# A two-layer linear-attention and gated-ReLU kernel on one core: the order of its instructions as a table

## The chip, the core and the metric

The kernel runs on one core of a Trainium2 chip. The metric is the device time of one execution in microseconds (us). Five engines work side by side, each through its own queue in the order in which the program lists its instructions: TensorE (PE: matmuls and transposes; PEld is its weight load), VectorE (DVE), ScalarE (ACT), GpSimd (POOL) and SyncE (SP, which issues DMAs). Semaphores make an instruction wait for what it reads from another engine. TensorE writes to PSUM, the other operands lie in SBUF.

## The reference, cut to what matters

`x` is 2048 rows of 512 in bfloat16. Two equal layers follow one another, each an attention (A) and a gated unit (B):

```python
pq = einsum("bhsd,hdf->bhsf", q, w_phi)          # 32 heads of 16; the same for k
phi_q = concatenate([softmax(pq), softmax(-pq)]) # over the 16 features
kv  = einsum("bhsf,bhsd->bhfd", phi_k, v)
z   = einsum("bhsf->bhf", phi_k)
o   = (phi_q . kv) / ((phi_q . z) + 1e-6)
A   = o @ wo
gate = x @ W_gate; up = x @ W_up                 # 512 x 1376 each
B   = (where(gate > 0, gate, 0) * up) @ W_down
x = x + A(layernorm(x)); x = x + B(layernorm(x)) # twice, with the same weights
```

`kv` and `z` are sums over all 2048 rows, so no row's output of an attention can be formed before every row's keys are.

## The kernel before, in words

**Tiles.** The rows are 16 tiles of 128, in 4 chunks of 4 tiles. `X` stays in SBUF as [128, 16, 512]. The feature map is folded into the projection: 4 folds each give `Wk2 = wk.Wblk` and `Wq2 = wq.Wblk` (L348; their inputs are turned by TensorE for keys and by DMA, L334, for queries; L304 and L306 take the results from PSUM on ScalarE or VectorE, by letters of a table).

**A layer.** `Norm` (L367 on) normalises a chunk in groups of tiles: statistics on VectorE (L385, L387), a few small steps on GpSimd that end in a power of -0.5 (L393, L395, L442, L444), the normalisation on ScalarE (L456) or on VectorE or GpSimd (L468), and the turn of the rows, by TensorE (L477), by DMA for two tiles at once (L482) or for one (L486). In a chunk whose sums come free with the addition to `X` (L494), ScalarE squares instead (L408). `keys_values` then does per tile the keys (L637), exponentials of p and -p (L642), the values (L590), the sums over 16 features (`feature_sums`: one reduction of the whole tile L609, two of half a tile L619, or an addition on GpSimd L606 and a reduction of the half L615), a reciprocal (L651), the product with it (L657, cut between GpSimd and VectorE), and the matmuls into `kv` (L679). `build_R` (L701) spreads `kv` into a block matrix. `queries` does the same for q: L721, L725, the feature sums, a reciprocal of the second sums (L730), the product `rq` of the two sums (L732), the rescale of half the tile with it (L739, GpSimd or VectorE), and a DMA transpose on SP (L741). `attention` does per tile the matmuls called er (L758, into the kind of buffer `q`), a reciprocal (L776) and the division (L778) on VectorE, which free `q`, the turn of the quotient (L785 and L791 by DMA, L798 by TensorE), the projection with `wo` (L809) and the addition to `X`. `glu` does the remainder of 96 features (L520, L525, L527, L530), 10 slices of gate and up (L540), their evacuations and products (L546, L550, L553, L557), and the down-projection (L572) with the addition and, in layer 1, the output (L577).

**What sets the order.** Nothing is issued while the code above runs. `Plan.op` records each operation (1888 in all) with its engine, a cost, what it reads and writes, a latency `lat` and an earliest time `at`. `order` then simulates the engines: at every moment each free engine takes, of its ready operations, the one with the highest sum of rank (the longest way to the end) and bias; the bias comes from the table `RANK`, a base and a slope per kind of operation and engine. An operation flagged `long` (GpSimd's larger ones) keeps those flagged `port` (VectorE's L468, L557, L657, L739) from being placed while it runs. Buffers come from kinds with a fixed count (`ps` 6 and `q` 1 in PSUM; `b2` 32, `b4` 6, `b1` 26 and smaller ones in SBUF); an operation that needs a buffer waits in the plan until one is free. `emit` (L176 on) issues the operations in that order under a manual schedule, so that each engine's queue is fixed by it, and the semaphores follow from the data.

**Tables.** `STEP` (L817) chooses per tile or chunk by letters: which engine evacuates, which form of sums is used, how many of the 8 groups of L657 GpSimd takes, whether a turn is done by TensorE or DMA.

**Loads.** `setup` issues the first two tiles of `X` on SP and the rest of `X`, `wkv`, `wq` and `w_phi` on ACT's queue (L224 to L239). `load_weights` (L297) plans 28 pieces of `wo`, `wr`, `wg`, `wu` and `wd` on SP, none before the plan's time 13.0. `wake` (L315) puts 17 matmuls of zeros at TensorE's start. L265 builds a small 0/1 matrix by a reduction of the identity on VectorE.

Of the kernel before, what the change touches and what calls it, by code (L numbers as in the profile page):

```python
# [60 lines left out]
class Plan:  # L61
# [10 lines left out]
    def op(self, eng, occ, fn, reads=(), writes=(), holds=(), lat=0.0, at=0.0, group=None, port=False, long=False):  # L72
# [4 lines left out]
        base, slope = RANK.get(f"{o.group}.{eng}") or RANK[o.group]  # L77
        o.bias = base - slope * o.i_in
# [19 lines left out]
    def order(self):  # L98
        for o in self.ops:
            for p in o.preds:  # L100
                p.succs.append(o)
        for o in reversed(self.ops):
            o.rank = o.cost + o.lat + max([s.rank + hop(o.eng, s.eng) for s in o.succs], default=0.0)
        free = {k: [0.0] * n for k, (pool, n) in self.kinds.items()}
        engines = sorted({o.eng for o in self.ops})
        busy = {e: 0.0 for e in engines}
        ready = {e: [] for e in engines}
        for o in self.ops:
            o.wait, o.t0 = len(o.preds), o.at
            if not o.wait:  # L110
                ready[o.eng].append(o)
        seq, left, now, shut = [], len(self.ops), 0.0, 0.0
        while left:
            moved, later = False, []
            for e in engines:
                if busy[e] > now + 1e-9:
                    later.append(busy[e])
                    continue
                best = None
                for o in ready[e]:  # L120
                    if o.t0 > now + 1e-9:
                        later.append(o.t0)
                        continue
                    if o.port and shut > now + 1e-9:
                        later.append(shut)
                        continue
                    ok = True
                    need = {}
                    for b in o.bufs:
                        if b.slot is None:  # L130
                            need[b.kind] = need.get(b.kind, 0) + 1
                    for k, n in need.items():
                        got = [t for t in free[k] if t is not None]
                        if len(got) < n:
                            ok = False
                        else:
                            t = sorted(got)[n - 1]
                            if t > now + 1e-9:
                                later.append(t)
                                ok = False  # L140
                    if ok and (best is None or (o.rank + o.bias, -o.i) > (best.rank + best.bias, -best.i)):
                        best = o
                if best is None:
                    continue
                o = best
                ready[e].remove(o)
                moved, left = True, left - 1
                o.start, end = now, now + o.cost
                busy[e] = now + o.occ
                if o.long:  # L150
                    shut = end
                later.append(busy[e])
                for b in o.bufs:
                    if b.slot is None:
                        b.slot = min((i for i, t in enumerate(free[b.kind]) if t is not None),
                                     key=lambda i: free[b.kind][i])
                        free[b.kind][b.slot] = None
                        b.end = 0.0
                    b.left -= 1
                    b.end = max(b.end, end + o.lat + FREE)  # L160
                    if not b.left:
                        free[b.kind][b.slot] = b.end
                for s in o.succs:
                    s.wait -= 1
                    s.t0 = max(s.t0, end + o.lat + hop(e, s.eng))
                    if not s.wait:
                        ready[s.eng].append(s)
                seq.append(o)
            if not moved:
                later = [t for t in later if t > now + 1e-9]  # L170
                assert later, "the plan is stuck"
                now = min(later)
        self.seq = seq
        return seq
# [15 lines left out]
WF_IN, WK_IN, WV_IN, WQ_IN, LOADED = 3.5, 5.9, 8.6, 13.1, 13.0  # L190
X_IN = [3.25, 3.8] + [7.0] * 2 + [10.1] * 4 + [11.6] * 4 + [14.5] * 4
# [8 lines left out]
def setup(ctx, tc, A_x, A_wqkv, A_w_phi, A_wo, B_W_gate, B_W_up, B_W_down, out):  # L200
# [64 lines left out]
    nc.vector.tensor_reduce(out=st.M4[:], in_=ident[:].rearrange("p (k h) -> p h k", h=4), axis=AX.X, op=Alu.max)  # L265
    st.Wblk = const.tile([P, NDB, P], BF16, name="Wblk")
# [24 lines left out]
def load_weights(st):  # L291

    nc, seen = st.nc, {}
    for n, (name, dst, src, kb) in enumerate(st.loads):
        i = seen[name] = seen.get(name, -1) + 1
        st.pl.rank("ld" if name == "wd" else "l", n)
        st.pl.op("SP", max(0.45, kb / 245.0), lambda dst=dst, src=src: nc.sync.dma_start(out=dst, in_=src), writes=[(name, i)], at=LOADED, lat=2.0)  # L297
# [635 lines left out]
```

## Time and profile before

| | us |
|---|---|
| median of 3 runs (lowest to highest) | 382.19 (382.05 to 382.74) |
| the profiled execution's own time | 380.87 |
| its span | 379.1 |
| TensorE busy | 368.0 |
| VectorE busy | 272.1 |
| ScalarE busy | 211.0 |
| GpSimd busy | 139.5 |

The span runs from the first to the last instruction of the program in the trace; the execution's own time has 1.77 us more around it. The profiled execution is one run, and it lies below the three timed ones. "L758" is line 758 of the kernel before; `out<-in` names the buffers with their numbers left out (`b` stands for every `b1`, `b2`, `b4`). In a row of groups stand the engine, the operation, the shapes and the count, then the busy time, the mean length of one in ns, and the engine's idle time just before them with what ended it. In a row of waits stand the instruction that waited, what it waited for, the total, the count and the longest.

### The profile page before, as it was taken

Reading aid. Unit: us, or ns where it says so; the run is one execution under the profiler, and the core shown is the slowest. Engines: PE = TensorE matmul, PEld = TensorE weight load, DVE = VectorE, ACT = ScalarE, POOL = GpSimd, SP = SyncE. Lnnn points to the kernel's source line nnn. Section 1 sums busy time; section 2 is a strip of 40 time slices with the busy share of each in tenths; the row PEclk is TensorE's granted clock in tenths of the full one; section 3 lists DMA queues with packets and bytes.
Section 4 is the critical chain, followed back from the end, with each engine's and each line's share of the span. In section 5 each row is a group of like instructions: output and inputs, shape, how many; then the busy total and the mean of one; then the engine's idle time right before and its main releaser. Section 6 shows DMA issues by size and latency. Waiting matters only on the chain.

```text
span 379.1 us, 6873 instructions
## 1 busy us (share of the span) xinstructions
PE 368.0 (97%) x2435; PEld 190.8 (50%) x2435; DVE 272.1 (72%) x606; ACT 211.0 (56%) x436; POOL 139.5 (37%) x272
## 2 busy tenths in 40 slices
PE   8699999999999999999999999999999999999996
PEld 4245545666445454444454455576655444454444
DVE  5999999999789725636992688999985592532232
ACT  4899878752598241238476377986725135124600
POOL 3799876903366000134360446545311021000000
PEclk9899999999999999999999999999999999999999
DMA  8999816449585100141232020656977014020011
GB/s 255 252 219 212 211 39 138 47 91 173 96 153 100 29 15 2 28 57 29 47 52 55 3 55 2 124 104 86 164 153 112 0 28 112 0 28 30 1 43 55
DMA packets 98403, 32.23 MB, mean 85 GB/s; under 512 B 88800, under 2 KB 98368, under 8 KB 98368
## 3 DMA queue, kind: packets, MB, share of 16 engines
q1 hardware_dynamic: 94400, 28.36, 39.8%
q10 hardware_dynamic: 3968, 3.42, 2.9%
q8 instruction: 19, 0.31, 0.4%
q14 instruction: 16, 0.13, 0.1%
HBM read 8.44 MB, written 2.10 MB: 28 GB/s over the span
## 4 chain that ended last, share of the span: by engine, by line
PE 80%; DVE 9%; DMA 4%; POOL 4%; issue 1%; SPq 1%; ACT 0%; ACTq 0%; POOLq 0%
PE ps L540 36%; PE ps L572 19%; PE ps L809 6%; PE ps L721 4%; PE ps L590 4%; PE ps L637 3%; DMA b<-b 3%; PE ps L520 3%; PE q L758 2%; DVE sk L619 2%; POOL b L657 1%; PE ps L315 1%; DVE rk L651 1%; PE q L679 1%; DVE bnst L385 1%
## 5 line engine op out<-in xcount | busy, mean ns | idle before, releaser
L540 PE MATMUL ps<-b,wu 128*128 128x512 bf16 (+2 forms) x400 | 79.4, 337 | 0.0
L540 PE MATMUL ps<-b,wg 128*128 128x512 bf16 (+2 forms) x400 | 78.9, 337 | 0.0
L572 PE MATMUL ps<-wd,b 128*128 128x512 bf16 (+3 forms) x374 | 78.3, 367 | 0.0
L550 ACT CAST b<-ps 128x512 bf16<-128x512 f32 (+2 forms) x100 | 48.9, 505 | 40.6 <-PE ps L540 39.3
L553 DVE SCALAR_TENSOR_TENSOR b<-ps,b 128x512 bf16<-128x512 f32 (+2 forms) x60 | 34.9, 598 | 30.3 <-PE ps L540 29.8
L572 PEld LDWEIGHTS <-b 128*128 128x128 bf16 (+1 forms) x374 | 35.3, 98 | 39.4
L657 POOL TENSOR_TENSOR b<-b,rk 128x1024 bf16<-128x1024 bf16 (+6 forms) x30 | 42.1, 1410 | 33.9 <-DVE rk L651 26.0
L540 PEld LDWEIGHTS <-wg 128*128 128x128 bf16 x400 | 36.2, 98 | 32.9 <-issue 0.2
L540 PEld LDWEIGHTS <-wu 128*128 128x128 bf16 x400 | 36.1, 98 | 31.9
L456 ACT ACTIVATE b<-X,ve,rstd 128x512 bf16<-128x512 bf16 x42 | 33.4, 818 | 26.2 <-POOL ve L444 21.5
L739 POOL TENSOR_TENSOR b<-b,rq 128x512 bf16<-128x512 bf16 x25 | 26.3, 1050 | 31.2 <-DVE rq L732 24.2
L498 DVE TENSOR_TENSOR X<-X,ps 128x512 bf16<-128x512 bf16 (+2 forms) x34 | 22.0, 649 | 21.2 <-PE ps L572 20.6
L725 ACT ACTIVATE b<-ps 128x512 bf16<-128x512 f32 x64 | 33.3, 615 | 6.2 <-PE ps L721 6.1
L408 ACT ACTIVATE sq<-X 128x512 bf16<-128x512 bf16 x32 | 20.0, 626 | 28.5 <-DVE X L494 26.2
L637 PE MATMUL ps<-Wk,b 128*128 128x512 bf16 x128 | 31.5, 388 | 4.0 <-DMA b<-b 4.0
L642 ACT ACTIVATE b<-ps 128x512 bf16<-128x512 f32 x64 | 33.2, 612 | 1.2 <-PE ps L637 1.2
L494 DVE SCALAR_TENSOR_TENSOR X<-ps,X 128x512 bf16<-128x512 f32 x32 | 21.7, 684 | 13.4 <-PE ps L572 12.5
L809 PE MATMUL ps<-wo,b 128*128 128x512 bf16 x128 | 30.9, 379 | 0.1
L590 PE MATMUL ps<-wkv,b 128*128 128x512 bf16 x128 | 30.9, 384 | 0.0
L721 PE MATMUL ps<-Wq,b 128*128 128x512 bf16 x128 | 30.9, 379 | 0.0
L557 DVE TENSOR_TENSOR b<-b,b 128x512 bf16<-128x512 bf16 (+2 forms) x40 | 14.1, 373 | 22.3 <-ACT b L550 21.9
L546 ACT ACTIVATE b<-ps 128x512 bf16<-128x512 f32 (+2 forms) x40 | 19.8, 496 | 15.1 <-PE ps L540 15.1
(84 smaller groups left out, 463.8 us busy)
## 6 DMA issues: line engine op xcount, KB each, us to landing
out_dram<-X SPq DMA_DIRECT2D x15, 128.0 KB, 1.7
X<-in_A_x_dram ACTq DMA_DIRECT2D x3, 512.0 KB, 7.6
b<-b SPq DMA_TRANSPOSE x87, 3.2
wd<-in_B_W_down_dram SPq DMA_DIRECT2D x5, 256.0 KB, 3.2
wu<-in_B_W_up_dram SPq DMA_DIRECT2D x8, 160.0 KB, 3.3
wg<-in_B_W_gate_dram SPq DMA_DIRECT2D x8, 160.0 KB, 2.9
wkv<-in_A_wqkv_dram ACTq DMA_DIRECT2D x2, 512.0 KB, 5.1
wq<-in_A_wqkv_dram ACTq DMA_DIRECT2D x1, 512.0 KB, 8.3
```

The lines of the kernel that those rows point to most:

```text
L456: pl.op("ACT", 0.72, lambda to=to, t=t, j=j: nc.scalar.activation(out=to(), in_=st.X[:, t, :], func=AF.Identity, scale=rstd[:, j:j + 1], b ...
L540: nc.tensor.matmul(ps[:], lhsT=wt[:, b, f * P:(f + 1) * P], rhs=xnT[:, lo:hi, b, :], start=(b == 0), stop=(b == NDB - 1))
L550: pl.op("ACT", 0.065 + 0.42 * share, lambda ups=ups, ru=ru: nc.scalar.copy(out=ru[:], in_=ups[:]), reads=[(ups, 0)], writes=[(ru, 0)])
L553: pl.op("DVE", 0.08 + 0.53 * share, lambda gps=gps, ru=ru, h=h, cs=cs: nc.vector.scalar_tensor_tensor(out=h[:, cs], in0=gps[:], scalar=0.0 ...
L572: nc.tensor.matmul(yps[:], lhsT=hs[f][:fsz, ti * P:(ti + 1) * P], rhs=st.wd[:fsz, f, cols], start=(f == 0), stop=(f == NFT - 1))
L590: nc.tensor.matmul(vp[:], lhsT=xnT[:, ti, kb, :], rhs=st.wkv[:, kb, D:2 * D], start=(kb == 0), stop=(kb == NDB - 1))
L637: nc.tensor.matmul(ps[:], lhsT=xnT[:, ti, kb, :], rhs=w(kb), start=(kb == 0), stop=(kb == NDB - 1))
L642: pl.op("ACT", 0.49, lambda s=s, ek=ek, pk=pk: nc.scalar.activation(out=ek[:, :, s, :], in_=pk[:].rearrange("p (j x) -> p j x", j=8), func ...
L657: eng.tensor_tensor(out=phiK[:, lo:hi, :, :].rearrange("p j s (f h) -> p (j s) f h", h=4), in0=ek[:, lo:hi, :, :].rearrange("p j s (f h) - ...
L721: nc.tensor.matmul(pq[:], lhsT=xnT[:, ti, kb, :], rhs=st.Wq2[:, kb, :], start=(kb == 0), stop=(kb == NDB - 1))
L725: pl.op("ACT", 0.49, lambda s=s, eq=eq, pq=pq: nc.scalar.activation(out=eq[:, :, s, :], in_=pq[:].rearrange("p (j x) -> p j x", j=8), func ...
L809: nc.tensor.matmul(yps[:], lhsT=turned(b), rhs=st.wo[:, b, :], start=(b == 0), stop=(b == NDB - 1))
```

## The change

1. `RANK` and the simulation that chose the order are gone. `ORDER`, a table of 1888 numbers, says in which sequence the recorded operations are issued. The new `order` walks it, asserts that every operation stands behind what it depends on, and gives out buffers.
2. The costs recorded with the operations change: a GpSimd half addition 0.64 in place of 0.54, VectorE's reduction of its result 0.48 in place of 0.31, DMA transposes 2.0 and 2.8 in place of 1.85, a load 2.3 in place of 2.0, other arrival times of `X` and the weights. These numbers reach the chip only through the table and the choice of buffers.
3. The first chunk is normalised in groups of (1,1,1,1) tiles in place of (1,1,2): four normalisations with small steps of their own, and single transposes of tiles 2 and 3 in place of one for both.
4. Every weight piece is recorded as a reader of `("turns", 1)`, which the turn of tile 5 writes, so each stands behind that transpose on SP.
5. A third way to sum features ("T": the tile turned by DMA, then 8 matmuls with a 0/1 matrix `M8s`) is there, and `M8s` is built by one more reduction on VectorE; no letter of the tables chooses "T".
6. Tables `qm0` and `qm1` let GpSimd form the product `rq` of 4 of the 32 query tiles. Other tables change in single letters.

The core of the diff (the 1888 numbers and lines that only pass a name on are cut):

```diff
     def order(self):
...
+        assert sorted(ORDER) == list(range(len(self.ops)))
+        self.seq = [self.ops[i] for i in ORDER]
+        for o in self.seq:
+            assert o.preds <= seen
+            seen.add(o)
+            t = max([busy.get(o.eng, 0.0), o.at] + [p.end + hop(p.eng, o.eng) for p in o.preds])
+            for b in o.bufs:
+                if b.slot is None:
+                    b.slot = min((i for i, f in enumerate(free[b.kind]) if f is not None), key=lambda i: free[b.kind][i])
+                    t, b.end, free[b.kind][b.slot] = max(t, free[b.kind][b.slot]), 0.0, None
+            o.start = t = max(t, shut) if o.port else t
...
+    st.M8s = const.tile([P, 2, 4], BF16, name="M8s")
+    nc.vector.tensor_reduce(out=st.M8s[:], in_=ident[:].rearrange("p (z k h) -> p z h k", z=2, h=4), axis=AX.X, op=Alu.max)
...
-        st.pl.op("SP", max(0.45, kb / 245.0), lambda dst=dst, src=src: nc.sync.dma_start(out=dst, in_=src), writes=[(name, i)], at=LOADED, lat=2.0)
+        st.pl.op("SP", max(0.45, kb / 245.0), lambda dst=dst, src=src: nc.sync.dma_start(out=dst, in_=src), reads=[("turns", 1)], writes=[(name, i)], at=LOADED, lat=2.3)
...
-                        reads=[(both, 0), (both, 1)], writes=[(self.dst, ti - 1), (self.dst, ti)], lat=1.85)
+                        reads=[(both, 0), (both, 1)], writes=[(self.dst, ti - 1), (self.dst, ti)] + ([("turns", 1)] if self.at and t == 5 else []), lat=2.0)
...
+        by_pool = STEP["qm" + L][t] == "P" and how != "T"
+        pl.op("POOL" if by_pool else "DVE", 0.23 if by_pool else 0.19, lambda sq2=sq2, sums=sums, rq=rq, by_pool=by_pool: (
+            nc.gpsimd if by_pool else nc.vector).tensor_tensor(out=rq[:], in0=sq2[:, :, 1, :], in1=sums[:, :, 0, :], op=Alu.mult),
+            reads=[(sq2, 1), (sums, 0)], writes=[(rq, 0)])
...
 STEP = {
-    "part0": "4111", "part1": "4111", "tB0": "A---", "tB1": "D-DA", "tA": "----", "wev": "AADDAAADADAAAAAA",
+    "part0": "4111", "part1": "4111", "tB0": "A---", "tB1": "D-D-", "tA": "----", "wev": "AADDAAADAAAAAAAA",
...
-    "sB1": 2, "sA": 3, "xB0": "ADADAAAADADADDAA", "xB1": "DADAAADAAAAAAAAD", "xA": "AADDDDDADAADAAAA",
-    "xm0": "22222212", "xmB0": "22221122", "xmB1": "22222222", "xm1": "12222222", "om0": "11112222",
-    "om1": "11222222", "ev0": "AAAAAAAAAAAAAAAA", "ev1": "AAADAADAAAAAADAA", "ks0": "7888076880873788",
-    "ks1": "4322711876616443", "kr0": "H1111P1121221222", "kr1": "P12111111H12P222", "qr0": "1111H11P1122P1PP",
-    "qr1": "111P111111111112", "qs0": "PPPDPPPPDDDPDPPP", "qs1": "PPPPPPPDDPPPPPPP", "ot0": "DDDD-----DDDAA--",
-    "ot1": "--A---AD--A---D-",
+    "sB1": 3, "sA": 3, "xB0": "ADADDAADDADADDAA", "xB1": "DADAAADAAAAAAAAA", "xA": "ADDDDDDAAADDAAAA",
+    "xm0": "22222211", "xmB0": "22221122", "xmB1": "21222221", "xm1": "12211211", "om0": "11112222",
+    "om1": "11222222", "ev0": "AAAAAAAAAAAAAAAA", "ev1": "AAADAADAAAAAADAA", "ks0": "7888076880873788",
+    "ks1": "4325718366616443", "kr0": "H1111P1121222222", "kr1": "P11112111H122212", "qm0": "DDDDPDDDDDDDDDPD",
+    "qm1": "DDDDPDDDDPDDDDDD", "qr0": "2111H1122122P1PP", "qr1": "111P112112111112", "qs0": "PPPDPPPPPDDPDPPP",
+    "qs1": "PDPPPPPDDPPPPPPP", "ot0": "DDDD------DDAA--", "ot1": "--A--DAD--DA---A",
 }
-RANK = {
...
+ORDER = (
+    137, 139, 134, 144, 138, 136, 141, 131, 135, 146, 0, 129, 132, 1, 9, 145, 2, 143, 4, 3, 133, 147, 10, 5, 11, 6,
...
-        n = Norm(st, "b4", (1, 1, 2) if c == 0 else (2, 2), STEP["xn1"], STEP["xm0"], X_IN, STEP["turn"] if c == 0 else "")
+        n = Norm(st, "b4", (1, 1, 1, 1) if c == 0 else (2, 2), STEP["xn1"], STEP["xm0"], X_IN, STEP["turn"] if c == 0 else "")
```

How the table moves instructions on each engine can't be seen in the diff. VectorE's up to the sixth L778 are counted in the prediction. TensorE has ahead of the seventh L758 the same matmuls in both orders, but for four of L540 with 128x128 more in the new one. On SP the new order has three of the last weight pieces (of `wd`, `wg` and `wo`) behind the second transpose of L741, and the last piece of `wd` behind the seventh. The first chunk's transposes go in the order tile 2, tile 1, tile 3 (tile 0 is turned by TensorE).

## The prediction on record

> **What bounds the kernel now.** I read the page's shares first, then a table of five stretches, then the waits.
>
> ```profile
> PE 368.0 (97%) x2435; PEld 190.8 (50%) x2435; DVE 272.1 (72%) x606; ACT 211.0 (56%) x436; POOL 139.5 (37%) x272
> ...
> PE 80%; DVE 9%; DMA 4%; POOL 4%; issue 1%; SPq 1%; ACT 0%; ACTq 0%; POOLq 0%
> ```
>
> TensorE looks full over the whole span, and the chain of waits runs over it for 80%. So only the places where TensorE is not full can give time back, and the table of stretches says where they are (columns: length, busy time and instructions of each engine, granted TensorE clock, DMA).
>
> ```profile
> 0.00:20.00 20.00, 15.38 (x80) 6.91 (x81) 15.47 (x45) 12.92 (x22) 12.04 (x38) 0.91 0.92 250
> 20.00:75.00 55.00, 52.12 (x464) 28.79 (x463) 52.62 (x110) 47.96 (x101) 46.82 (x62) 1.00 0.70 145
> 75.00:98.00 23.00, 23.00 (x172) 13.93 (x169) 22.85 (x66) 8.46 (x20) 4.93 (x7) 1.00 0.72 133
> 98.00:376.00 278.00, 277.24 (x1728) 141.07 (x1727) 180.90 (x387) 141.69 (x295) 75.75 (x168) 1.00 0.32 58
> ```
>
> From 98 to 376 us TensorE is idle for 278.00 - 277.24 = 0.8 us. Nearly all of its idle time lies before 75 us: 4.6 us in the first 20 and 2.9 in the next 55. In that second stretch VectorE is busy 52.62 of 55.00 us, more than TensorE. The first layer's feature sums, their reciprocals and the divisions behind the er matmuls (L758) are VectorE's, and TensorE waits for them. TensorE's waits by stretch, the first two rows from 0 to 20 us, the next two from 20 to 75, the last from 98 on (total, times, longest):
>
> ```profile
> PE ps L637 <- DMA b<-b: 3.4, 2, 3.1
> PE ps L315 <- DVE zero L232: 1.2, 1, 1.2
> ...
> PE q L758 <- DVE b L778: 1.3, 2, 0.7
> PE q L679 <- POOL b L657: 1.2, 2, 0.7
> ...
> PE ps L637 <- DMA b<-b: 0.7, 1, 0.7
> ```
>
> The largest is the wait for tile 1's transposed rows, but it does not decide. Ahead of the first er, and again of the seventh, the program order of the old and of the new kernel has the same matmuls to within four. There is one q buffer, so an er waits for the division of the er before it, on a VectorE that has no slack. What TensorE gains before is waited away there, and the last such place is the seventh er:
>
> ```profile
> 73.12 1.50 PE L540 MATMUL ps<-b,wg 128*128 128x128 bf16 x24
> 74.77 0.43 PE L758 MATMUL q<-R,b 128*128 128x68 bf16 x8
> ```
>
> ```profile
> 73.14 0.68 DVE L778 TENSOR_TENSOR b<-q,dd 128x512 bf16<-128x512 f32 x1
> ```
>
> VectorE frees q at 73.14 + 0.68 = 73.82. The er starts at 74.77, when its transpose has landed (below). After it TensorE runs without a wait of note to the end, so a shift of this instruction is a shift of the end.
>
> **The change part by part.** *VectorE's work ahead of the seventh er.* I counted VectorE's instructions up to the sixth division (L778) in both program orders. The new one has, on balance, 1 reduction of the identity more (M8s), 8 half-tile sums L619 more, 1 reciprocal L730 more, and fewer: 1 whole-tile sum L609, 2 sums after a GpSimd add (L615), 1 product L732, 1 normalisation L468. It is the sums of about two tiles pulled forward, and split sums instead of whole ones. Groups of VectorE from 0 to 74 us (busy, mean ns):
>
> ```profile
> L385 DVE BATCH_NORM_STATS2 bnst<-X 128x6 f32<-128x512 bf16 x16 | 10.5, 668 | 0.3 <-DMA X<-in_A_x_dram 0.3
> L609 DVE TENSOR_REDUCE sq<-b 128x64 f32<-128x1024 bf16 x7 | 8.3, 1186 | 0.0
> L619 DVE TENSOR_REDUCE sk<-b 128x32 f32<-128x512 bf16 x13 | 8.2, 652 | 0.0
> L732 DVE TENSOR_TENSOR rq<-sq 128x32 bf16<-128x32 f32 x8 | 3.0, 373 | 0.0
> L730 DVE RECIPROCAL sq<-sq 128x32 f32<-128x32 f32 x8 | 2.6, 330 | 0.0
> L615 DVE TENSOR_REDUCE sq<-b 128x32 f32<-128x256 f32 x3 | 1.6, 537 | 0.0
> L468 DVE TENSOR_SCALAR b<-X,mv,rstd 128x512 bf16<-128x512 bf16 x4 | 1.6, 410 | 1.9 <-POOL rstd L395 1.9
> L265 DVE TENSOR_REDUCE M<-ident 128x4 bf16<-128x128 bf16 x1 | 0.3, 268 | 0.0
> ```
>
> 0.268 (M8s is not in the trace; its neighbour L265 reads the same identity) + 8 x 0.652 + 0.330 - 1.186 - 2 x 0.537 - 0.373 - 0.410 = **+2.8 us**. This speaks against the change.
>
> *VectorE's waits ahead of the seventh er.* From 0 to 74 us:
>
> ```profile
> DVE b L468 <- POOL rstd L395: 1.9, 3, 0.6
> DVE b L306 <- PE ps L348: 1.8, 1, 1.8
> DVE zero L232 <- PEq L917: 0.9, 1, 0.9
> DVE vext L261 <- issue: 0.8, 1, 0.8
> DVE b L468 <- POOL ve L444: 0.7, 1, 0.7
> DVE bnst L385 <- DMA X<-in_A_x_dram: 0.3, 1, 0.3
> DVE sk L615 <- POOL b L606: 0.2, 1, 0.2
> ```
>
> The 0.9 and 0.8 stand ahead of everything and stay. That leaves 4.9. The new order puts the identity's reductions ahead of the first statistics: the 0.3 goes. The first chunk by tile puts tile 2's statistics (0.67) into the 1.8: I take 0.7. Of the three L468 waits of 0.6, the first has three statistics between its producers and itself in the new order and goes (0.6). The one of 0.7 goes, since that normalisation stands behind the sixth division now. Of the other two and the 0.2 (1.4 together) I take half, 0.7, as the order does not settle them. Sum: 0.3 + 0.7 + 0.6 + 0.7 + 0.7 = **-3.0 us**, with 0 and -4.9 as its ends.
>
> *The held forms.* One product L732 alone takes 0.18, and 0.98, 0.59 and 0.55 when GpSimd runs:
>
> ```profile
> 51.73 0.98 DVE L732 TENSOR_TENSOR rq<-sq 128x32 bf16<-128x32 f32 x1
> ...
> 54.65 0.18 DVE L732 TENSOR_TENSOR rq<-sq 128x32 bf16<-128x32 f32 x1
> ...
> 56.10 0.59 DVE L732 TENSOR_TENSOR rq<-sq 128x32 bf16<-128x32 f32 x1
> ...
> 57.31 0.55 DVE L732 TENSOR_TENSOR rq<-sq 128x32 bf16<-128x32 f32 x1
> ```
>
> ```profile
> 50.75 1.91 POOL L657 TENSOR_TENSOR b<-b,rk 128x1024 bf16<-128x1024 bf16 x1 [0.43 <-DVE sq L730]
> ...
> 55.98 0.67 POOL L606 TENSOR_TENSOR b<-b 128x256 f32<-128x256 bf16 x1
> ```
>
> The first ends at 52.71, GpSimd's instruction at 52.66. Three holds cost 0.80 + 0.41 + 0.37 = 1.6 us. The table adds no wait to the program; it can only place these products between GpSimd's instructions. In the new order the third and fourth products still stand beside three GpSimd rescales in a row, so I take 0, with -1.6 as the other end. The Trainium skill ("SBUF — State Buffer", Who interferes with whom) says that a VectorE instruction with two SBUF inputs and a GpSimd one that reads SBUF exclude each other, and that the first to start blocks the other for its whole length. The 0.98 agrees. By that rule a good placement would save the 1.6, and the sum would be 3.1 instead of 1.5; a product that starts first makes GpSimd wait instead.
>
> *The seventh er.* VectorE is done with q at 73.82 + 2.8 - 3.0 = 73.6, and the er starts at 73.7 instead of 74.77 if its transpose is there: -1.1. The chain of waits shows that transpose behind GpSimd:
>
> ```profile
> 69.29 1.01 POOL b L739
> ...
> 70.32 4.40 DMA b<-b
> ```
>
> GpSimd's small normalisation steps and half-sums that ran between the sixth and the seventh rescale stand behind it in the new order, so it starts well over 1.1 us earlier. If not, the 1.1 is lost and 0.4 of gain stays. TensorE has four L540 of 128x128 more done by then, and over the whole program four transposes fewer (last tile of tB1); four of that size take 0.22:
>
> ```profile
> 63.62 0.22 PE ps L798 x4
> ```
>
> So -0.2 and -0.2. **Sum: -1.1 - 0.2 - 0.2 = -1.5 us.**
>
> *Edits at nothing.* The start: tiles 2 and 1 are sent first, singly; whatever it saves of the 3.4 us is covered by the waits for VectorE, as said. The weight pieces: held behind tile 5's transpose, which takes one load out from between tile 1's and tile 2's; in exchange the last piece of wd stands on SP behind the seventh q transpose. Landing takes 3.2 and the first use is at 77.57:
>
> ```profile
> wd<-in_B_W_down_dram SPq DMA_DIRECT2D x5, 256.0 KB, 3.2
> ```
>
> ```profile
> 77.57 2.38 PE ps L572 x11
> ```
>
> Even behind a transpose issued at 70.32 and taking its 1.2 of issue, it lands at 74.8, 1.3 us ahead of a use moved to 76.1. Without that cover each us late is a us lost. The sums by a turned tile ("T") are reached by no letter of the tables, so they cost M8s alone. The planner's new costs act only through the table. From 98 us on everything is reshuffled, but TensorE idles 0.8 us there and VectorE 97: I take 0, bounds -0.8 and +0.8 (the wait of 0.7 again).
>
> **The rivals.**
> 1. *VectorE gets later, slower.* Place: the divisions before the seventh er. The 2.8 us of added work come surely, the 3.0 of saved waits are half argued. With savings s, the end moves by 1.5 - s. Below s = 0.7 the kernel is slower; at s = 0 it is +1.5, 383.7 us. For it: VectorE has no idle reserve from 20 to 98 us. Against: three of the waits have a named filler.
> 2. *Eaten, no change.* s from 0.7 to 2.2: 381.4 to 383.0. The start's gain would show and vanish at the ers.
> 3. *The holds go too.* s = 4.9 and the 1.6: 1.5 - 6.5 = -5.0, 377.2 us. For it: the order is a free choice per instruction. Against: rescales in a row.
> 4. *A weight piece late.* wd beyond the 1.3 us of margin: 1 us late beyond it gives 380.7 + 1.0 = 381.7, 3 us 383.7.
> 5. *It does not do what it says*: the holds stay, since nothing in the program waits. That is in the forecast already.
>
> **How the numbers follow.** The profiled execution took 380.87 us, span 379.1 and 1.77 around it; the sum gives 379.4. The median of the runs is 382.19, 1.3 above; the same -1.5 gives **380.7 us**. Measurement of this kernel tells about 0.2%, 0.76 us, from no change. Chances: forecast 0.42, rival 3 and what lies towards it 0.18, rival 2 0.18, rival 1 0.18, rival 4 0.04. Faster 0.60, same 0.18, slower 0.22. Range: from near rival 3's end to rival 1's end, 377.4 to 383.7, which also holds the 0.8 either way of the later stage.
>
> **What would show it.** Right: VectorE's wait of 1.8 near 7 us halved, L468 waits under 1 us in total before 74 us, the seventh er near 73.7, a product L694 still stretched beyond 0.5 us somewhere between 50 and 60 us. Wrong: the seventh er after 75 us (rival 1), before 72 (rival 3), a wait of the first down-projection for a DMA (rival 4), or TensorE waits of more than 1.5 us after 98 us, for which nothing here has a price.

## The result and the profile after

The changed kernel takes **383.66 us** (median of 20 runs, 382.27 to 384.59), the kernel before, beside it, 382.24 us (20 runs, 380.55 to 383.78). The ratio is 1.0038, with a 95% interval of 1.0026 to 1.0051: it is slower by 0.38%, or 1.4 us, where 380.7 us and a gain were forecast. The profiled execution of the new kernel took 384.05 us (span 382.1), that of the kernel before 380.87. The two traces thus lie 3.2 us apart, more than the kernels do: the one of before is one of its faster executions. A second trace of each, from experiments e1 (before) and e13 (new), stands beside the first where a reading needs it. Of the 1.4 us, 0.17 lies outside the span: execution time less span is 1.89 us in the mean of the new kernel's 20 runs and 1.73 in that of 29 runs of the kernel before. No run shows why.

One figure ahead has to be mended: the kernel before records 1880 operations, the new one 1888.

From the profile of the new kernel, busy times and shares of the chain of waits:

```profile
PE 367.7 (96%) x2398; PEld 190.6 (50%) x2431; DVE 269.8 (71%) x605; ACT 207.4 (54%) x441; POOL 140.9 (37%) x280
...
PE 76%; DVE 10%; ACT 4%; DMA 3%; issue 2%; POOL 2%; ACTq 1%; SPq 0%; DVEq 0%; POOLq 0%
```

TensorE's busy time can't be compared to a us: 2398 matmuls are recorded beside 2431 weight loads, so 33 are missing from this trace, mostly after 98 us. Its waits can be compared. In the first 20 us (the two longest rows), from 20 to 76 (three) and from 98 on (all four), total, times and longest:

```profile
PE ps L536 <- DMA b<-b: 2.1, 1, 2.1
PE ps L261 <- DVE zero L176: 1.2, 1, 1.2
...
PE q L637 <- POOL b L615: 1.5, 1, 1.5
PE ps L423 <- ACT b L402: 1.1, 1, 1.1
PE ps L771 <- DMA wo<-in_A_wo_dram: 0.6, 1, 0.6
...
PE q L637 <- POOL b L615: 0.7, 1, 0.7
PE ps L595 <- DMA b<-b: 0.4, 1, 0.4
PE ps L486 <- DVE b L499: 0.3, 1, 0.3
PE q L720 <- DVE b L740: 0.2, 1, 0.2
```

The 3.1 for a transposed tile became 2.1, and the waits of the ers for the division are gone from this list. In their place stand three that the kernel before did not have at that size: the key sums L637 for GpSimd's last rescale (L615), the turn of a tile L423 for its normalisation, and the first projection L771 for a piece of `wo`. From 98 us on the waits add up to 1.6 us, where the kernel before had one of 0.7 in both of its traces. The new kernel's second trace has the same four there and one more, 2.4 us in all:

```profile
PE ps L771 <- DMA b<-b: 0.9, 1, 0.9
```

VectorE up to the start of the sixth division, as stretches of the trace of before (first fence) and of the new one (second; length, then busy PE, PEld, DVE, ACT, POOL):

```profile
0.00:73.14 73.14, 65.79 (x512) 34.16 (x513) 66.23 (x151) 60.30 (x120) 57.00 (x94) 0.98 0.77 176
```

```profile
0.00:75.81 75.81, 67.24 (x511) 34.58 (x520) 69.03 (x157) 59.74 (x119) 57.59 (x98) 0.98 0.74 171
```

VectorE's busy time, the third behind the length, grew by 69.03 - 66.23 = 2.80 us, as counted. Its idle time was 73.14 - 66.23 = 6.91 and is 75.81 - 69.03 = 6.78. But ScalarE starts 0.8 us later in this trace of the new kernel (7.45 beside 6.66; the first experiment shows the rows), and a late start lengthens VectorE's idle time. So the second traces are needed beside the first, up to the same division, of before (first fence) and of the new kernel (second):

```profile
0.00:74.98 74.98, 65.17 (x504) 33.92 (x513) 66.51 (x152) 60.19 (x120) 57.07 (x94) 1.00 0.76 171
```

```profile
0.00:74.93 74.93, 66.37 (x519) 34.25 (x520) 69.45 (x156) 59.58 (x119) 57.51 (x98) 1.00 0.74 173
```

VectorE is idle 8.47 and 5.48 us in these. ScalarE's queue has issued its last load at 6.62 and 7.75 us in the two traces of before, at 7.40 and 6.37 in those of the new kernel. Idle time less that moment is 0.29 and 0.72 before, -0.62 and -0.89 now. An estimate from these four traces: VectorE saved about 1.3 us of waits (0.9 to 1.6), while its busy time grew by 2.5 to 3.2. VectorE's six longest waits from 0 to 76 us in the new kernel's first trace:

```profile
DVE bnst L331 <- DMA X<-in_A_x_dram: 1.9, 1, 1.9
DVE sk L566 <- ACT b L600: 1.5, 2, 1.1
DVE zero L176 <- PEq L951: 0.9, 1, 0.9
DVE M L209 <- POOL hr L233: 0.7, 1, 0.7
DVE X L440 <- PE ps L771: 0.4, 1, 0.4
DVE Wblk L270 <- DMA wf<-in_A_w_phi_dram: 0.4, 1, 0.4
```

All four waits of its normalisations (1.9 and 0.7 before) are gone, and so is the 1.8 for turned weights (L348). But VectorE, ahead of its data now, waits 1.9 for the rows of tile 2 and 1.5 for the exponentials of keys. In the second trace, with its earlier start, these two are 0.7 and 0.8.

The seventh er and the division before it, in the new kernel's rows of TensorE and of VectorE:

```profile
77.17 0.42 PE L720 MATMUL q<-R,b 128*128 128x68 bf16 x8
```

```profile
75.81 0.67 DVE L740 TENSOR_TENSOR b<-q,dd 128x512 bf16<-128x512 f32 x1
```

`q` is free at 76.48, and the er starts 0.7 after that, at 77.17. So in this trace the division is no longer the last thing it waits for; TensorE itself arrives late, after the three waits above. The second traces, of before (first fence) and of the new kernel (second), put the same er at:

```profile
76.84 0.43 PE L758 MATMUL q<-R,b 128*128 128x68 bf16 x8 [0.39 <-DVE sq L609]
```

```profile
76.30 0.42 PE L720 MATMUL q<-R,b 128*128 128x68 bf16 x8
```

Counted from the end of ScalarE's last load issue, this er starts after 68.15 and 69.09 us in the kernel before and after 69.77 and 69.93 in the new one, in the mean 1.2 more. From the er to the end of the span it is 304.33 and 304.06 us before, 304.93 and 305.90 now, in the mean again 1.2 more. So the new kernel is late on both sides of the seventh er. The three waits ahead of the er have these causes, each in the row that shows it. VectorE, GpSimd and TensorE around 50 us, in the first trace:

```profile
50.12 1.09 DVE L694 TENSOR_TENSOR rq<-sq 128x32 bf16<-128x32 f32 x1
51.13 0.54 DVE L609 RECIPROCAL rk<-sk 128x64 bf16<-128x64 f32 x1
```

```profile
51.84 1.91 POOL L615 TENSOR_TENSOR b<-b,rk 128x1024 bf16<-128x1024 bf16 x1 [0.68 <-PE ps L536]
```

```profile
53.80 0.43 PE L637 MATMUL q<-vext,b 128*128 128x68 bf16 x8 [1.47 <-POOL b L615]
64.12 0.59 PE L771 MATMUL ps<-wo,b 128*128 128x512 bf16 x2 [0.56 <-DMA wo<-in_A_wo_dram]
71.78 0.40 PE L423 MATMUL ps<-ident,b 128*128 128x128 bf16 x4 [1.10 <-ACT b L402]
```

A product of queries is held by GpSimd to 1.09 (0.18 alone). The last keys' reciprocal stands behind it and starts at 51.13, the last rescale at 51.84, and TensorE waits 1.47 for it. (The last two of TensorE's rows are the other two waits.) The piece of `wo` was issued on SP behind the second transpose of queries:

```profile
59.56 2.44 SPq L243 DMA_DIRECT2D wo<-in_A_wo_dram  x1
```

It arrives 64.12 - 59.56 = 4.6 us after the start of its issue, where the median piece of `wo` takes 3.1. The kernel before had sent all of `wo` by 46 us. And on GpSimd a half addition (L552, 68.61 to 69.28) stands between small steps of a normalisation, whose last (L390) ends at 70.88; ScalarE's normalisation follows at 70.92.

### The profile page after: what moved, and what is told of

Same layout as the page of the kernel before. It is cut to its first block, busy times and chain, and to the rows that moved or that the text cites. A ratio compares the mean times of both kernels' runs of the same rounds, so it can differ in the third digit from the quotient of the medians.

```text
span 382.1 us, 6760 instructions
## 1 busy us (share of the span) xinstructions
PE 367.7 (96%) x2398; PEld 190.6 (50%) x2431; DVE 269.8 (71%) x605; ACT 207.4 (54%) x441; POOL 140.9 (37%) x280
## 4 chain that ended last, share of the span: by engine, by line
PE 76%; DVE 10%; ACT 4%; DMA 3%; issue 2%; POOL 2%; ACTq 1%; SPq 0%; DVEq 0%; POOLq 0%
PE ps L486 32%; PE ps L518 19%; PE ps L771 6%; PE ps L595 5%; PE ps L536 4%; PE ps L679 4%; PE ps L466 2%; DVE sk L576 2%; PE q L720 2%; DMA b<-b 2%; ACT b L600 1%; DVE rk L609 1%; DVE sq L566 1%; DMA wo<-in_A_wo_dram 1%; ACT b L402 1%
## 5 line engine op out<-in xcount | busy, mean ns | idle before, releaser
L496 ACT CAST b<-ps 128x512 bf16<-128x512 f32 (+2 forms) x100 | 47.5, 506 | 71.0 <-PE ps L486 70.9
L615 POOL TENSOR_TENSOR b<-b,rk 128x1024 bf16<-128x1024 bf16 (+7 forms) x30 | 43.5, 1456 | 26.6 <-issue 11.9
L499 DVE SCALAR_TENSOR_TENSOR b<-ps,b 128x512 bf16<-128x512 f32 (+2 forms) x60 | 33.3, 592 | 25.1 <-PE ps L486 14.8
L600 ACT ACTIVATE b<-ps 128x512 bf16<-128x512 f32 x64 | 35.6, 614 | 7.4 <-PE ps L595 7.0
L683 ACT ACTIVATE b<-ps 128x512 bf16<-128x512 f32 x64 | 34.0, 622 | 8.7 <-PE ps L679 7.7
L536 PE MATMUL ps<-wkv,b 128*128 128x512 bf16 x122 | 31.9, 387 | 2.5 <-DMA b<-b 2.1
L354 ACT ACTIVATE sq<-X 128x512 bf16<-128x512 bf16 x36 | 22.8, 634 | 21.0 <-DVE X L440 18.9
L444 DVE TENSOR_TENSOR X<-X,ps 128x512 bf16<-128x512 bf16 (+2 forms) x30 | 19.2, 648 | 20.9 <-PE ps L518 17.8
L595 PE MATMUL ps<-Wk,b 128*128 128x512 bf16 x125 | 32.7, 387 | 1.2 <-ACT Wk L250 0.5
L771 PE MATMUL ps<-wo,b 128*128 128x512 bf16 x120 | 31.0, 379 | 0.9 <-DMA wo<-in_A_wo_dram 0.6
L361 POOL TENSOR_SCALAR u<-mv 128x2 f32<-128x2 f32 (+1 forms) x22 | 5.1, 234 | 68.3 <-DVE X L440 67.9
L440 DVE SCALAR_TENSOR_TENSOR X<-ps,X 128x512 bf16<-128x512 f32 x36 | 24.0, 679 | 8.3 <-PE ps L518 7.3
```

What stands on the lines that cost most here:

```text
L496: pl.op("ACT", 0.065 + 0.42 * share, lambda ups=ups, ru=ru: nc.scalar.copy(out=ru[:], in_=ups[:]), reads=[(ups, 0)], writes=[(ru, 0)])
L499: pl.op("DVE", 0.08 + 0.53 * share, lambda gps=gps, ru=ru, h=h, cs=cs: nc.vector.scalar_tensor_tensor(out=h[:, cs], in0=gps[:], scalar=0.0 ...
L536: nc.tensor.matmul(vp[:], lhsT=xnT[:, ti, kb, :], rhs=st.wkv[:, kb, D:2 * D], start=(kb == 0), stop=(kb == NDB - 1))
L595: nc.tensor.matmul(ps[:], lhsT=xnT[:, ti, kb, :], rhs=w(kb), start=(kb == 0), stop=(kb == NDB - 1))
L600: pl.op("ACT", 0.49, lambda s=s, ek=ek, pk=pk: nc.scalar.activation(out=ek[:, :, s, :], in_=pk[:].rearrange("p (j x) -> p j x", j=8), func ...
L615: eng.tensor_tensor(out=phiK[:, lo:hi, :, :].rearrange("p j s (f h) -> p (j s) f h", h=4), in0=ek[:, lo:hi, :, :].rearrange("p j s (f h) - ...
```

## The experiments

Two theories stood at the start. **A**: the loss is made ahead of the seventh er, by VectorE's added work and three places of the order that its chain passes. **B**: it is spread over the program, second half included, or lies in the changed start. "Old order" below is the order that the kernel before has, read off and written as a table; moves are of single operations in `ORDER`.

### The kernel before once more

No edit.

> The kernel before once more, unchanged, for a second trace. Its first traced execution took 380.87 us, 1.4 below the median of 20 runs (382.24). If the first trace was a lucky execution, this one shows waits of TensorE before the first er that the first does not show, and an execution near 382.2; if the traces of before are alike, it shows the same waits to 0.2 us each and an execution near 380.9.

It took 382.61, 1.74 more than the first trace of the same kernel. ScalarE's queue, its first normalisation and TensorE's last key sums, in the first trace of before:

```profile
5.33 1.29 ACTq L239 DMA_DIRECT2D X<-in_A_x_dram  x1
6.66 0.81 ACT L456 ACTIVATE b<-X,ve,rstd 128x512 bf16<-128x512 bf16 x1 [2.77 <-POOL ve L444]
```

```profile
52.72 0.43 PE L679 MATMUL q<-vext,b 128*128 128x68 bf16 x8 [0.54 <-POOL b L657]
```

and in the second:

```profile
4.41 1.97 ACTq L238 DMA_DIRECT2D wq<-in_A_wqkv_dram  x1
6.42 1.33 ACTq L239 DMA_DIRECT2D X<-in_A_x_dram  x1
7.80 0.81 ACT L456 ACTIVATE b<-X,ve,rstd 128x512 bf16<-128x512 bf16 x1 [3.92 <-POOL ve L444]
```

```profile
53.89 0.43 PE L679 MATMUL q<-vext,b 128*128 128x68 bf16 x8 [0.55 <-POOL b L657]
```

ScalarE starts 0.04 and 0.05 after its queue has issued its last load. The issue of `wq` took 1.97 in place of 0.98, so ScalarE was 1.14 later, the last key sums 1.17, the seventh er 2.07, the end 1.74. In six traces with the old order up to there the last key sums start 46.10 to 46.14 after the end of that issue. A late start thus arrives at 53 us undiminished, and in the kernel before it reaches the end: a good part of its spread of some 1 us either way can come from there. The new kernel has 46.40 and 46.56 in two traces. Its first factor is ready on GpSimd at 6.13, ScalarE's queue ends at 7.40:

```profile
6.14 1.26 ACTq L183 DMA_DIRECT2D X<-in_A_x_dram  x1
7.45 0.81 ACT L402 ACTIVATE b<-X,ve,rstd 128x512 bf16<-128x512 bf16 x1 [3.55 <-issue]
```

So up to 0.8 of the 3.2 us between the first two traces can be this spread in the start, not the change. It isn't shown for the end, though: the new kernel's second trace (e13) starts ScalarE at 6.42, 1.03 earlier, has the seventh er 0.87 earlier, and takes 384.08 us, as long as the first with 384.05.

### The three places, singly

```diff
+ORDER = list(ORDER)
+for i, j in ((351, 365), (375, 344)):       # e2: two products
+for i, j in ((127, 116), (114, 127), (103, 114)):  # e3: wd, wg, wo ahead of the transposes
+for i, j in ((452, 501),):                  # e4: half addition behind the normalisation
+    ORDER.remove(i)
+    ORDER.insert(ORDER.index(j) + 1, i)
```

> The new kernel with two of VectorE's products rq moved: that of tile 0 (held 0.88 us behind a GpSimd rescale at 50.1 us) behind the second whole-tile sum that follows the last key reciprocal, that of tile 3 (held 0.6 us) behind the second half of R. Theory H (the held products are what made the new order late): the last key reciprocal ends 0.9 us earlier, TensorE's wait of 1.66 us for the last GpSimd rescale of the keys shrinks to about 0.7, the first er starts 0.9 to 1.2 us earlier, and the kernel takes 383.7 - 1.0 = 382.7 us or less. Rival G (the gain is waited away at the following ers, which VectorE's work ahead of the seventh division sets): the first er is earlier and the eighth is not; 383.7 us, no change. Rival M (each of TensorE's waits is a cost of its own) agrees with H here.

> The new kernel with the three weight pieces that stand behind the second transpose of a query tile on SP (one each of wd, wg, wo) issued before the first of them, where SP has nothing else to do for 8 us. TensorE's wait of 0.54 us for wo goes. Rival M (each wait is a cost of its own): the eighth er and the end come 0.5 us earlier, 383.2 us. Theory G (VectorE's work ahead of the divisions sets the end): TensorE waits 0.5 us more elsewhere before the eighth er, 383.7 us.

> The new kernel with one half addition of GpSimd (for query tile 12) taken from between the small steps of the first normalisation of the unit and put behind them. Those steps end 0.65 us earlier and TensorE's wait of 1.29 us for the first turned tile shrinks to about 0.65. Rival M: the end comes 0.6 us earlier, 383.1 us. Theory G: waited away, 383.7 us.

Against before on the same chip: e2 1.0038 (1.0017 to 1.0060), e3 1.0035 (1.0017 to 1.0054), e4 1.0023 (1.0006 to 1.0039). Each did its work in the trace. TensorE's wait for the last rescale in e2 is half:

```profile
52.73 0.43 PE L637 MATMUL q<-vext,b 128*128 128x68 bf16 x8 [0.75 <-POOL b L615]
```

In e3 there is no wait for `wo`, and in e4 the normalisation's is 0.5 in place of 1.1. But in e3 the next one grew:

```profile
PE ps L423 <- ACT b L402: 1.4, 1, 1.4
```

The trace of e3 also has 1.06 in place of 0.37 for transposed rows at 107 us. In e4 TensorE waits 1.8 for transposed rows, but at 21 and 32 us, far ahead of the instruction that was moved; the new kernel's second trace has such a wait of 1.4 at 21 us too, so it is not the edit's. That one of the three places carries the loss is not borne out: the intervals of all three overlap the new kernel's, and e4, the lowest, gives back 0.15% by its middle value, some 0.6 us. Of that, 0.17 us lies outside the span: execution time less span is 1.88 and 1.92 in the means of e2 and e3, and 1.72 in e4, as in the kernel before.

### Where the loss lies: parts of one order and parts of the other

The lines say what the tables hold; in the runs the tables are written out, with the numbers that the letters of each part give.

```diff
-ORDER = (...)                # the new one
+ORDER = NEW[:920] + [i for i in OLD if i not in NEW[:920]]   # e5; e7 with 330, e15 with 540
+ORDER = OLD[:905] + [i for i in NEW if i not in OLD[:905]]   # e6
```

In all four, weight pieces are not held to tile 5's turn.

> The new table and letters up to the last er of layer 0 (the first 920 of its operations), then the rest in the order and with the letters of the kernel before; weight pieces not held, M8s kept. In the traces so far TensorE's idle time after about 160 us is 2.0 to 2.2 us with the old order and 3.4 to 3.5 with the new. Theory L (the second half of the new table loses about 1.3 us, and the first half loses little on balance): 383.7 - 1.3 + 0.2 (four transposes return) = 382.6 us, near the kernel before (382.2). Rival E (the loss lies wholly in the first half, at the keys' last sums and the ers, as the prediction's first rival has it): 383.7 us.

> The other way round: the order and letters of the kernel before up to the last er of layer 0 (905 operations), then the new ones. Theory L: 382.2 + 1.3 - 0.2 = 383.3 us. Rival E: 382.2 - 0.2 = 382.0 us.

> The new table and letters for the first 330 operations only, which is up to the last key tile's sums, with the first chunk normalised by single tiles; all the rest as before. Theory S (a gain at the start is carried to the end, since VectorE is shifted with it): TensorE's idle time up to tile 14 of the keys was 10.8 and 12.0 us in the two traces of before and 10.6 to 11.0 in four of the new order, so this kernel takes 382.2 - 0.7 = 381.5 us. Rival of the prediction (whatever the start saves is covered by the waits for VectorE): 382.2 us, no change.

> The new table and letters up to the seventh er (540 operations), then the old order and letters; weight pieces not held. Theory Q (the loss arises ahead of the seventh er, the place the prediction names): 1.4 us above the kernel before. Rival R (it arises behind it, between the seventh er and the last): 0 to 0.4 above.

New up to the last er of layer 0 (e5): 1.0041 (1.0018 to 1.0065). New up to the seventh er (e15): 1.0028 (1.0009 to 1.0047). Old up to the last er of layer 0 and new from there (e6): 1.0009 (0.9988 to 1.0030). By e6 the new second half costs 0.3 us, and at most 1.1. A loss as large as the whole is there with the new first half alone, and about half of it with the new order up to the seventh er (on that chip the new kernel itself stands at 1.0055). That speaks against the part of B that puts the loss in the second half.

The seams limit this. e7 (new only up to the 330th operation) gave 1.0031 (1.0010 to 1.0052), but its seam makes a wait of 2.0 at the last key sums that neither kernel has, so it decides nothing about the start. e5 and e15 have such waits too: from 98 us on TensorE waits 2.2 us in e5 and 1.95 in e15 (for transposed rows 1.43 and 0.50; 1.14 and 0.81), where the kernel before has 0.7. So they do not show, as A has it, that the loss arises ahead of the seventh er. In their traces that er starts 69.06 and 69.34 us after ScalarE's last load issue, little later than in the second trace of before, and from it to the end it is 305.73 and 305.17 us, over 1 us more than there.

### The four edits together

e2, e3 and e4 in one, and one letter that takes less of the last tile's rescale to GpSimd in layer 1:

```diff
-    "ks1": "4325718366616443",
+    "ks1": "4325718366616441",
+for i, j in ((351, 365), (375, 344), (127, 116), (114, 127), (103, 114), (452, 501)):
```

> The new kernel with four edits together: the two products moved, the three weight pieces early, the half addition behind the first normalisation's small steps, and the last key tile of layer 1 cut 1 to 7 in place of 3 to 5 between GpSimd and VectorE (its GpSimd part takes 0.40 in place of 1.08 us, VectorE's 0.15 us more). Rival M (each wait is a cost of its own): 0.9 + 0.5 + 0.65 + 0.45 = 2.5 us, 383.7 - 2.5 = 381.2 us. Theory G (waited away, since VectorE's work sets the end): 383.7 us. Half of it, 382.4, if the waits in the stage of the ers cover one another.

> The new kernel once more, so that the next three stand beside it on one chip. 1.4 us above the kernel before (383.7 beside 382.2).

> The new kernel with the four edits once more (two products, three weight pieces, the half addition, the cut of the last key tile). The first time it stood 0.3 to 0.4 us above the kernel before and the products alone 1.4 above it. Theory P (the waits in the stage of the ers cover one another, so that only all edits together bring time back): 0.9 us less than the new kernel beside it. Rival: the first measurement was chance; within 0.3 us of the new kernel.

e8: 1.0017 (0.9998 to 1.0035). On another chip the new kernel (e13) had 1.0055 (1.0034 to 1.0077) and the four edits (e14) 1.0027 (1.0011 to 1.0042). On that chip the medians of e13 and e14 lie 0.85 us apart. Together the edits give back 0.2 to 0.3%, about half of the loss, with intervals that overlap; 0.17 us of it lies outside the span (1.90 in e13, 1.73 in e14). e4 alone stood at 1.0023, no worse than the four in e14, so it is not shown that the waits covered one another. The seventh er of e14, and TensorE's three longest waits from 20 to 76 us:

```profile
75.81 0.42 PE L720 MATMUL q<-R,b 128*128 128x68 bf16 x8
```

```profile
PE ps L595 <- ACT vext L250: 1.2, 1, 1.2
PE q L637 <- POOL b L615: 0.7, 1, 0.7
PE ps L423 <- ACT b L402: 0.5, 1, 0.5
```

ScalarE's first normalisation is as late as in the new kernel's trace (7.47 beside 7.45), so its er at 75.81 in place of 77.17 is 1.4 us gained at that place. Of this the span keeps 0.2 (381.9 beside 382.1): from 98 us on TensorE waits 2.7 us in place of 1.6. In these two traces most of what was gained ahead of the seventh er was waited away behind it. The kernel still does not beat the one before.

### The start

e12 undoes the chunk by tile and keeps the new order:

```diff
-        n = Norm(st, "b4", (1, 1, 1, 1) if c == 0 else (2, 2), ...
+        n = Norm(st, "b4", (1, 1, 2) if c == 0 else (2, 2), ...
```

> The new kernel with one part undone: the first chunk normalised in groups of (1,1,2) again, the pair's steps standing where tile 3's stood and the pair's transpose behind tile 1's. The prediction's term (tile 2's statistics fill 0.7 us of VectorE's wait near 7 us) says that this costs 0.7 us: 384.4 us. Rival (in the new trace VectorE waits 1.87 us there for tile 2's rows themselves, so nothing is filled): no change, 383.7 us, or faster by the few GpSimd steps that are saved, 383.4 us.

388.05 us, 1.0160 (1.0133 to 1.0187), 4.4 above the new kernel's median. In e12, TensorE's row that waits for transposed rows:

```profile
18.04 1.89 PE L536 MATMUL ps<-wkv,b 128*128 128x512 bf16 x4 [5.98 <-DMA b<-b]
```

The wait is 6.0 in place of 2.1, and the 3.9 more arrive at the end in full. In an order that counts on single tiles, a later start is nowhere covered.

e9, e10 and e11 take the loads of `wq` and of `X`'s last chunk from ScalarE's queue to SP's, in the kernel before, the new one, and the new one with the four edits:

```diff
+    nc.scalar.copy(out=wq[:, 0, 0:1], in_=st.zero[:, 0:1])
...
-    nc.scalar.dma_start(out=wq[:], in_=wv[:, :, 0:D])
-    nc.scalar.dma_start(out=X[:, 12:16, :], in_=xv[:, 12:16, :])
+    nc.sync.dma_start(out=wq[:], in_=wv[:, :, 0:D])
+    nc.sync.dma_start(out=X[:, 12:16, :], in_=xv[:, 12:16, :])
```

> The kernel before with the last two loads of ScalarE's queue (wq and tiles 12 to 15 of X) issued by SP instead, behind a one-element copy on ScalarE that keeps them from starting before 3.9 us. In the traces so far ScalarE's first normalisation starts only when its queue has issued the last of these loads, at 6.6 us in one execution of the old order and at 7.4 and 7.8 in two others, and TensorE's idle time at the end of layer 0's keys is that moment plus 4.9 us in all three. Theory A (this issue is what sets the start and what spreads the runs): ScalarE is free at 5 us, the normalisation starts at 6.6 when GpSimd has its factor, every execution is like the fastest, 381.2 us, with a narrower spread. Rival: the two loads arrive at another time and the start is set by them, 382.2 or later.

> The new kernel with the same two loads on SP. In the new order GpSimd has the first factor at 6.1 us, 0.4 earlier than in the old one, and ScalarE was not free before 6.8 to 7.6. Theory A: the first normalisation starts at 6.2, TensorE's idle time at tile 1 shrinks by up to 1.2, but the waits that follow (last key sums, first turned tile) have own causes: 383.7 - 0.7 = 383.0 us. Rival G (VectorE's work sets the pace from 20 us on): 383.7 us.

> The four edits (two products, three weight pieces, the half addition, the cut of the last key tile) and the two loads on SP, on the new kernel. If both gains add: 382.6 - 0.7 = 381.9 us. If the start's gain is waited away: 382.6 us.

All lost: 1.0057 (1.0033 to 1.0082), 1.0116 (1.0087 to 1.0144), 1.0072 (1.0047 to 1.0096). The copy was to hold both loads; it held `wq` alone, and SP's queue in e9 issues `X`'s last rows third, at 1.71 us, and `wq` at 3.99, so the rows of the last tiles go ahead of data needed sooner. That this made the loss is not shown.

In e9 ScalarE's first normalisation still started at 6.79, now behind GpSimd's factor. This says nothing on what an earlier ScalarE would be worth.

### One held product, in the old order

```diff
 # the kernel before with its order as a table, product 343 behind 357
+ORDER.remove(343)
+ORDER.insert(ORDER.index(357) + 1, 343)
# e18 also: the products of tiles 1, 2 and 3 on GpSimd
+    "qm0": "DPPPDDDDDDDDDDDD",
```

> The old order, written as a table, with one product rq moved: that of tile 0, held 0.80 us by a GpSimd rescale at 51.7 us, one whole-tile sum later, when GpSimd is idle. Nothing else differs. Theory V (VectorE's work and stalls ahead of the ers are the clock): the 0.80 is saved, 382.2 - 0.8 = 381.4 us. Rival (covered by other waits): 382.2 us.

> The old order with the product of tile 0 one sum later, once more. The first time it stood 0.15% below the kernel before (interval -0.31 to +0.01%), while in its trace the next product (54.3 us) is held 0.53 in its place and the seventh er comes only 0.1 us earlier against ScalarE's last load issue. If the gain is real: 381.2 us or less, 0.7 below the kernel before. If it was chance: 382.0 to 382.3.

> The same, and the products of tiles 1, 2 and 3 formed by GpSimd itself (letters of the new table qm0), which cannot be held by GpSimd. They took VectorE 0.71, 0.59 and 0.57 us in the trace of the kernel with the one product moved; GpSimd has 0.25 us more for each. Theory V (VectorE's stalls ahead of the ers set the end): VectorE 1.9 us less ahead of the first ers, of which 1 us or more reaches the end: 380.4 us or less. Rival (GpSimd's three rescales, each behind one more instruction, or TensorE's other waits take it back): 381.2 us or above.

e16: 380.97, 0.9985 (0.9969 to 1.0001); e17, the same again: 382.00, 0.9992 (0.9968 to 1.0015). e18: 1.0016 (0.9992 to 1.0039). None is told apart from no change. VectorE's products in e16:

```profile
53.51 0.17 DVE L692 TENSOR_TENSOR rq<-sq 128x32 bf16<-128x32 f32 x1
54.30 0.71 DVE L692 TENSOR_TENSOR rq<-sq 128x32 bf16<-128x32 f32 x1
```

The moved one takes 0.17 where the first product took 0.98 before, and the next, which took 0.18 before, takes 0.71. In e18, with the three that follow it on GpSimd, VectorE waits for them:

```profile
56.85 0.61 DVE L570 TENSOR_REDUCE sq<-b 128x32 f32<-128x256 f32 x1 [0.86 <-POOL b L550]
58.40 0.87 DVE L699 TENSOR_TENSOR b<-b,rq 128x512 bf16<-128x512 bf16 x1 [0.35 <-POOL rq L692]
```

The hold is passed on, or turned into a wait, as long as GpSimd has one rescale after another.

## Why the prediction was wrong, point by point

- **VectorE's work, +2.8 us: right in sum.** The first pair of traces has +2.80 of busy time, the others 2.5 to 3.2. About 0.55 of the 2.80 is longer holds of the products, so the counted work came to about 2.25; that the two make up the sum is luck.
- **VectorE's waits, -3.0 us: this is the step that failed first.** The four traces give about -1.3, less than half. The named waits did go, more of them than forecast. The step took a wait that loses its cause for time that is gained, and did not ask what VectorE meets next. Tile 2's statistics, named as the filler of the 1.8 near 7 us, had to wait 1.9 and 0.7 for their own rows from memory, and pulled-forward sums of keys 1.5 and 0.8 for their exponentials. "No idle reserve from 20 to 98 us" stood in the prediction as the word for rival 1, and should have had the greater chance.
- **Held forms, 0: near.** Up to the division about 2.1 in place of 1.6 us; over the program what the products took above 0.19 rose from 3.41 to 4.40. The planned placing held more, not less, and one hold of 1.09 stood ahead of the last keys' reciprocal, on the chain.
- **The seventh er, 73.7 and so -1.1: some +1.2 by the four traces.** It came at 77.17 and 76.30, past the 75 named as the mark of rival 1. But the mark does not tell the kernels apart: the kernel before has 74.77 and 76.84. Rival 1's price at s = 0 is 383.7 us, and 383.66 was measured. That is luck: with the 1.3 us that VectorE did save, its sum gives 382.4. The rest came with TensorE's own lateness, at this er and behind it, for which rival 1 has no term.
- **"A shift of this instruction is a shift of the end", and 0 from 98 us on: the second step that failed.** It holds for the kernel before, whose two traces have 304.33 and 304.06 us from the seventh er to the end. In the new one it is 304.93 and 305.90, though TensorE has less work there (the -0.2 and -0.2 of the sum), and the trace with the earlier er ends no earlier. TensorE's waits from 98 us on are 1.6 and 2.4 us in place of 0.7. The sign that the prediction could not price, more than 1.5 us of them, came true. e6 alone, old up to the last er, has +0.09%, or 0.3 us, with an interval of -0.5 to +1.1, which fits the forecast's 0.8 either way for the new second half by itself.
- **The start "covered": wrong for a later start.** e12 shows 3.9 us of lateness arriving in full, and in the kernel before a start 1.1 us later made the end 1.7 later. Whether an earlier start is gained is open: 1.03 us earlier in the new kernel's second trace brought nothing at the end.
- **Weights, 0 with 1.3 of margin: right for `wd`, which nobody waits for; missed for `wo`**, 0.56 and 0.66 in the traces and, undone alone, nothing that can be measured. Rival 4 did not occur.
- **M8s, 0.27**, is part of the 2.80; it stands where VectorE waits 0.4 for `w_phi` anyway.

Shown by timed runs: the new kernel is slower by 0.38%; the new first half with the old second is as slow as the whole; the new second half alone costs at most 1.1 us; the four edits together give back about half by the middle values. Read from traces only: some 1.2 us ahead of the seventh er and as much behind it. In the mean of two traces each the kernels lie 2.3 us apart, more than their medians, so these are shares and not prices. Open: whether VectorE's added work alone makes the er late; what makes TensorE wait more behind it, for GpSimd's last rescale of layer 1 (0.66 us), for rows turned by DMA (0.37, and 0.86 more in the second trace) and for VectorE (0.29 and 0.24); why 0.17 us lies outside the span; and what the new start would give with ScalarE free at 6.1 us.

## What to carry to other kernels

A wait that vanishes from an engine's list is no gain until the next instructions in its queue have their data: follow the queue forward to the first instruction that would wait for something else, and count that. Where several engines are nearly full, follow a repair to the end of the program too: here, in one pair of traces, 1.4 us gained at one instruction left 0.2 at the end. Before two traces are subtracted, compare where their first dependent instructions start; one trace of each kernel can differ by more than the change.

## What the runs showed of the hardware

- ScalarE's first normalisation starts 0.04 to 0.05 us after its own queue's last DMA issue in all 17 traces that keep these loads on its queue. The issue of the same 512 KB load of `wq` took 0.98, 1.28, 1.64 and 1.97 us in four of them, and ScalarE started between 6.42 and 7.92 us. In the latest of these (e17) it was the issue of `X`'s last rows that took long, 2.39 us.
- A hold of VectorE's product beside GpSimd's rescales did not vanish when the product was moved: 0.98 became 0.17 and the next product went from 0.18 to 0.71. The Trainium skill ("SBUF — State Buffer", Who interferes with whom) says that the two exclude each other; the traces agree, and show besides that the second one in the row inherits the hold.
